# Moving the routing products, the shifted sums and the offset loads in an attention, expert and feed-forward kernel

## The chip, the cores and the metric

The kernel runs on one core of one Trainium2 chip, in one launch. The metric is device time in microseconds (us) of the whole program. Five engines work side by side and wait for one another by semaphores: TensorE (PE, matrix products and transposes; PEld is its weight load), VectorE (DVE), ScalarE (ACT), GpSimd (POOL) and SyncE (SP, which here only issues DMA transfers). A name like PEq, ACTq or SPq is the sequencer of an engine, which issues DMAs and handles registers. PSUM is the memory that PE writes; the kernel uses eight banks of it, tiles of 128 x 512 numbers of 4 bytes.

## The reference

Three steps, each on the output of the one before. Attention, for 4 batches of 8 heads with 576 rows and 64 columns each:

```
s_pos = maximum(s, 0); cum = cumsum(s_pos)
scores = q k^T / 8 + minimum(-(cum_i - cum_j), 0), causal
out = softmax(scores) v
```

Then a routed layer on x, the 2304 tokens of 512 numbers: `logits = x @ w_gate` (8 experts), each token goes to the expert with the greatest logit, `y = gate * (relu(x @ w1[e]) @ w2[e])`, where gate is that expert's softmax share. Then `h = max(y @ m1, y @ m2, y @ m3)` and `out = h @ w_out` for all tokens.

## The kernel before

**Attention** goes over 16 pairs of heads, four pairs to a batch. A pair takes 25 slots of a table (SEQ), and three pairs are in work at once: pair p has its score products (units s0 to s9, line 308, into the banks ps_a, of which there are four, used in turn), pair p-1 its transposes (A0 to TT, line 374, banks ps_b) and its products with the values (v0, v1, line 426, banks ps_c), pair p-2 its rows of the token matrix (x0, x1, lines 459 and 464, tile xr). DVE adds the bias to a score bank and takes the row's extremum (line 314, tile ns), ACT takes the exponential (line 321, tile P), and POOL masks the bias beforehand (line 269).

**The bias** of a pair (tile bl) is made of the running sum cum, shifted. For pair 0 PE spreads cum over the partitions by products with chl, the high and low part of cum (line 236), and the shift is done on DVE and ACT (lines 251 to 255). For all other pairs DVE makes the shifted sums cs once (line 569), SP writes them to DRAM (cumd, lines 575 and 578) and reads them back for each pair, spread over 64 partitions (line 218).

**Routing** of batch b (`route`) starts when the last pair of the batch has its token rows. It is a list C of short operations, one after another: the logits, the greatest (mx), its index (idx), the one-hot matrix oh and its bf16 copy ohb; then products r1 that count, for each token, the tokens before it in its group (bank from ps_a, result read as r_rv); then the place of each token (dd, bb, cbo, caA), and products r3 that put the token numbers in order (bank from ps_a, read into gidx). For the first three batches the list is laid between the attention of later pairs. For the last batch it lies between products of the expert layer, its banks are from ps_b, and its indices gi (line 781) are what POOL's gathers of the routed rows (tile xw, line 915) wait for.

**The expert layer** goes by nine groups of up to 336 tokens. Weights come by SP into tiles wr and xr and are split in a high and a low part (lines 192 and 685). The first three weight tiles are loaded, rounded and split during attention, at places set by WE0, WE1, WES and WEL. Group 0 holds tokens of the first three batches only and fills the time in which the last batch is routed; group 1 needs the gather. The results of groups after 0 go into yT at an offset that ACT holds in registers, loaded by line 793 from offi (`load_offs`).

**The order of the work** is written by hand: every operation is put on one list with `at(slot, fn)`, `atm(us, fn)` being the same by microseconds after the start of group 1, and run_events emits them by rising slot. The slot sets only the order on each engine, and no time: an engine takes its instructions in that order and waits at each for what it needs. `route` puts operation i at `t0 + (RS, RS, RS2, RSL)[b] * i`, that is 1.8, 1.8, 1.6 and 0.6 slots apart.

Of the kernel before, what the change touches and what calls it, by code (L numbers as in the profile page):

```python
# [14 lines left out]
AF = mybir.ActivationFunctionType  # L15
ALU = mybir.AluOpType
# [4 lines left out]
IT = 25  # L21
B, H, S, D = 4, 8, 576, 64
NT, DM, NE, DF, DF2 = B * S, H * D, 8, 1024, 768
P = 128
# [33 lines left out]
BW = 2112  # L58
CST, COT, L1 = -53, -42, -59
T0, T1, T2, T3, T4 = -56, -56, -53, -51, -43  # L60
# [5 lines left out]
MA, MB, MT = 8, 0.5, 0  # L66
RS = 1.8
CL = 26
# [8 lines left out]
WRB, R0, R1, XR, XQ = 3, 3, 2, 2, 1  # L77
WHI = "A"
WLO = "V"
WE0, WE1, WES, WEL, WEH = -62, 80, 46, 3, "A"  # L80
WHE, WLE = "A", "V"
SLOT = 0.456
# [6 lines left out]
LSEQ = "A0 B0 y0 y1 A1 B1 C2 v0 C3 TT . v1 . . x0 x1"  # L89
LS0, LSP, X14, RSL, RS2 = 1, 1.0, 8, 0.6, 1.6  # L90

# [7 lines left out]
def emit(nc, tc, qt, kt, v, s, wg, w1, w2, m64, out, dbg=None):  # L99
    V, A, G, T, SP = nc.vector, nc.scalar, nc.gpsimd, nc.tensor, nc.sync  # L100
# [55 lines left out]
    eio = iota_f([P, 5, NE], [[0, 5], [1, NE]], 0, 0, "eio")  # L156
# [3 lines left out]
    for b in (0, B - 1):  # L160
        t = cp.tile([P, 5, NG], F32, name=f"gx{b}")
# [40 lines left out]
    def at(slot, fn, *args):  # L202
        heapq.heappush(evq, (slot, next(seqno), fn, args))
# [271 lines left out]
    def route(b, t0):  # L475
        z = {}

        def sm(shape, nm, dt=F32):
            z[nm] = ab.tile(shape, dt, tag="r_" + nm, name="r_" + nm, bufs=1)
            return z[nm]  # L480

        b3 = lambda ap: bc(ap.rearrange("p (t o) -> p t o", o=1), (P, 5, NE))
# [3 lines left out]
        C = []  # L486
        op = C.append
# [7 lines left out]
        op(lambda: V.tensor_reduce(sm([P, 5], "mx"), z["L"], AX.X, ALU.max))  # L495
        op(lambda: V.tensor_tensor(sm([P, 5, NE], "ls"), z["L"], b3(z["mx"]), ALU.subtract))
        op(lambda: V.tensor_scalar(sm([P, 5, NE], "val"), z["ls"], 0.0, -float(NE), ALU.is_equal, ALU.mult))
        op(lambda: V.tensor_tensor(z["val"], z["val"], eio, ALU.add))
        op(lambda: V.tensor_reduce(sm([P, 5], "idx"), z["val"], AX.X, ALU.min))
# [14 lines left out]

        C[-1] = lambda: A.activation(sm([P, 5, NE], "ex"), z["ls"], AF.Exp)
        op(r1)
# [20 lines left out]
        def r3():  # L537
            pg = z["pg"] = bank("b" if b == B - 1 else "a")
            for t in range(5):
                T.matmul(pg[:, 0:NGW], z["cbo"][:, t, :], caA[:, NG * NWIN * t:NG * NWIN * t + NGW],  # L540
                         start=(t == 0), stop=(t == 4))

        op(r3)
        op(lambda: V.tensor_tensor(gidx, gidx, z["pg"][:, 0:NG * NWIN], ALU.add))
        if b == B - 1:
            op(lambda: to_idx())

        op(lambda: V.tensor_reduce(sm([P, NG], "os"), oh.rearrange("p t e -> p e t"), AX.X, ALU.add))
        op(lambda: V.tensor_tensor(ocar, ocar, z["os"], ALU.add))
# [3 lines left out]
        op(lambda: V.reciprocal(gtA[:, b], z["se"]))  # L553
        for i, f in enumerate(C):
            at(t0 + (RS, RS, RS2, RSL)[b] * i, f)
        return t0 + (RS, RS, RS2, RSL)[b] * (len(C) - 1)

    pos = {u: x / SLOT for u, x in SEQ.items()}
# [27 lines left out]
    for p in range(NP):  # L586
        t = IT * p
# [25 lines left out]
        if p == NP - 1 - H // 2:  # L613
            TR2 = end
    TA = IT * NP + 4
    TX = max(e[0] for e in evq) + 1
# [3 lines left out]
    def atm(us, fn, *args):  # L620
        at(TM + us / SLOT, fn, *args)
# [23 lines left out]
    t = TE  # L645
    S0, SL = [], []
    for x, gs in enumerate(STEPS):
        if x == NEARLY:
            t = TM
# [110 lines left out]
    for n in range(24):  # L760
        dst = w32 if n < 18 else wo32
        i, x = divmod(n if n < 18 else n - 18, 2)
# [14 lines left out]
    def early_idx():  # L777
        V.tensor_copy(gie, gidx[:, 0:NEARLY * NWIN])

    def to_idx():  # L780
        V.tensor_copy(gi, gidx)
# [109 lines left out]
    XG1 = max(TR2, TA) + 0.2  # L891
    at(TR2 + 0.1, early_idx)
    at(TX + 4, counts)
    at(TX + 8, load_offs)

# [100 lines left out]
    for x, gs in enumerate(STEPS):  # L996
# [7 lines left out]
        for g in gs:  # L1004
            L = cost[g]
            t0 = S0[x] - 1.3 / SLOT - st_ * (4 * len(gs) - m)
# [6 lines left out]
            for kk in range(4):  # L1013
                t = t0 + st_ * kk
# [12 lines left out]
            for d_ in range(4):  # L1027
                t = pt(g, 4 + d_)
# [210 lines left out]
```

## Time and profile before

| | |
|---|---|
| median of 3 runs | 795.99 us (795.22 to 797.65) |
| profiled execution | 794.54 us |
| its span, first to last instruction | 792.8 us |
| mean granted clock of TensorE | 0.995 of full |
| attention, until its last product (line 459) | about 213 us of the span |

The rows below are from that one execution. A timeline row gives the start, the busy time, engine, line, operation with its tiles, and in brackets how long the engine was idle before it and what ended that wait. Starts are in us from the first instruction. A wait is put down to the operation that came last. In a row of windows the granted clock (PEclk) is a share of 2.4 GHz.

### The profile page before, as it was taken

What the parts mean: (1) busy time and instruction counts of PE and PEld (TensorE: products, weight loads), DVE (VectorE), ACT (ScalarE), POOL (GpSimd) and SP (SyncE); (2) the same over time, 40 slices, a digit from 0 to 9 for tenths busy, and PEclk for the clock granted to TensorE, in tenths of its full rate; (3) what the DMA queues carried; (4) which work ended last, traced back from release to release, by engine and by line L of the source; (5) the groups of instructions that cost most, each with busy time, mean ns of one, the idle gap of its engine ahead of it and who ended that gap; (6) DMA issues with size and microseconds to landing.
All of it is one profiled execution on the core that took longest, in us unless ns stands there. A gap on an engine that the chain in (4) does not pass through costs nothing. (4 is left out here: it accounts for less than half of the span.)

```text
span 792.8 us, 12891 instructions
## 1 busy us (share of the span) xinstructions
PE 758.3 (96%) x4782; PEld 681.6 (86%) x4782; DVE 437.1 (55%) x1142; ACT 335.2 (42%) x771; POOL 109.4 (14%) x226
## 2 busy tenths in 40 slices
PE   6999899999889999999999999999999999999996
PEld 4666666666789998999999999989999899898995
DVE  5667757678668686899888756412312223122120
ACT  5666666666546343555455544221121212212111
POOL 3332332333030200101200000010010000100001
PEclk9999999999999999999999999999999999999999
DMA  5887858767386687868776535000010000100001
GB/s 154 238 216 217 212 160 225 194 181 222 135 281 210 221 310 256 308 221 281 238 230 214 204 97 172 26 31 10 1 41 1 26 14 1 41 1 14 26 1 41
DMA packets 34876, 112.43 MB, mean 142 GB/s; under 512 B 4793, under 2 KB 4875, under 8 KB 32891
## 3 DMA queue, kind: packets, MB, share of 16 engines
q1 hardware_dynamic: 24107, 81.66, 34.6%
q10 hardware_dynamic: 7456, 18.89, 6.7%
q0 software_dynamic: 3248, 11.03, 4.1%
q8 instruction: 39, 0.64, 0.3%
q14 instruction: 26, 0.21, 0.1%
HBM read 94.97 MB, written 16.60 MB: 141 GB/s over the span
## 5 line engine op out<-in xcount | busy, mean ns | idle before, releaser
L1135 DVE TENSOR_TENSOR mA<-ps_a,mA 128x384 f32<-128x384 f32 x72 | 40.2, 558 | 181.4 <-PE ps_a L942 181.4
L942 PE MATMUL ps_a<-yc,wq 128*128 128x384 f32 x720 | 129.1, 339 | 0.0
L942 PEld LDWEIGHTS ps_a<-yc,wq 128*128 128x128 f32 x720 | 127.4, 188 | 0.4
L942 PE MATMUL ps_c<-h,wq 128*128 128x336 f32 (+1 forms) x672 | 106.2, 316 | 3.1 <-ACT yT L988 1.6
L942 PEld LDWEIGHTS ps_c<-h,wq 128*128 128x128 f32 x672 | 101.8, 192 | 3.8 <-ACT yT L988 2.0
L942 PE MATMUL ps_a<-yc,wm 128*128 128x384 f32 x576 | 103.7, 339 | 0.0
L942 PE MATMUL ps_a<-xT,wq 128*128 128x336 f32 (+1 forms) x648 | 101.0, 313 | 1.1 <-DVE h L967 1.1
L942 PEld LDWEIGHTS ps_a<-yc,wm 128*128 128x128 f32 x576 | 101.9, 188 | 0.0
L942 PEld LDWEIGHTS ps_a<-xT,wq 128*128 128x128 f32 x648 | 96.5, 188 | 1.7 <-DVE h L967 1.4
L321 ACT ACTIVATE P<-ns,mn 128x512 f32<-128x512 f32 (+3 forms) x128 | 70.6, 558 | 14.9 <-DVE mn L314 14.7
L942 PE MATMUL ps_c<-wm,g 128*128 128x512 f32 x324 | 76.9, 396 | 0.0
L1139 ACT ACTIVATE g<-mA 128x384 fp32r<-128x384 f32 x36 | 18.9, 526 | 135.7 <-DVE mA L1135 135.7
L942 PEld LDWEIGHTS ps_c<-wm,g 128*128 128x128 f32 x324 | 60.9, 188 | 14.4
L1158 POOL DMA_INDIRECT out<-o,midi x18 | 17.5, 973 | 378.1 <-ACT o L1154 373.9
L314 DVE CUSTOM_DVE_ANT_0 ns<-ps_a,bl 128x512 f32<-128x512 f32 (+3 forms) x128 | 57.5, 488 | 19.5 <-PE ps_a L308 8.1
L685 DVE TENSOR_TENSOR wq<-wr,wq 128x1024 fp32r<-128x1024 f32 x44 | 53.9, 1226 | 10.4 <-ACT wq L192 9.7
L426 PEld LDWEIGHTS ps_c<-ptT,nv 128*64 128x64 f32 x448 | 29.8, 138 | 31.5 <-DVE ptT L414 13.3
L426 PE MATMUL ps_c<-ptT,nv 128*64 128x320 f32 (+4 forms) x448 | 51.4, 367 | 5.4 <-DVE ptT L414 5.2
L192 ACT ACTIVATE wq<-wr 128x1024 fp32r<-128x1024 f32 x44 | 46.3, 1056 | 17.9 <-DMA wr<-in_w 17.9
L308 PE MATMUL ps_a<-nk,nq 64*128 64x512 f32 (+3 forms) x256 | 47.0, 472 | 3.4 <-DVE mn L314 1.8
L374 PE MATMUL ps_b<-idf,P 128*128 128x128 f32 x320 | 47.1, 284 | 2.0 <-DVE ptT L414 1.2
L963 ACT ACTIVATE h<-ps_a 128x336 fp32r<-128x336 f32 (+1 forms) x64 | 28.0, 440 | 46.0 <-PE ps_a L942 45.4
(221 smaller groups left out, 953.5 us busy)
## 6 DMA issues: line engine op xcount, KB each, us to landing
wr<-in_w SPq DMA_DIRECT2D x49, 512.0 KB, 4.8
bl<-cumd SPq DMA_DIRECT2D x30, 528.0 KB, 9.1
dr<-in_m ACTq DMA_DIRECT2D x24, 512.0 KB, 4.5
xr<-in_w SPq DMA_DIRECT2D x23, 512.0 KB, 4.8
nq<-in_qt SPq DMA_DIRECT2D x16, 352.0 KB, 3.7
nv<-in_v SPq DMA_DIRECT2D x16, 320.0 KB, 9.5
nk<-in_kt SPq DMA_DIRECT2D x16, 288.0 KB, 2.9
xd<-xr SPq DMA_DIRECT2D x4, 1152.0 KB, 6.5
```

What stands on the lines that cost most here:

```text
L192: A.activation(o, x, AF.Copy)
L308: T.matmul(d["sp", i, g][:, :w], d["q"][r, 128 * i:128 * i + 128], d["k"][r, :w], start=True, stop=True)
L314: V.tensor_tensor_reduce(out=ns[:, :w], in0=d.pop(("sp", i, g))[:, :w], in1=d["bl"][:, 1024 * g + BOFF[i]:1024 * g + BOFF[i] + w], scale=- ...
L321: A.activation(pp, d.pop(("ns", i, g))[:, :w], AF.Exp, bias=d["mn"][:, c:c + 1], scale=-1.0, accum_out=ssum[b][:, i, h + g:h + g + 1])
L374: T.transpose(pt[:, c:c + 128], (d["P", "t"] if g == "t" else d["P", g, i])[:, k0:k0 + 128], idf)
L426: T.matmul(po[64 * g:64 * g + 64, qa - c0:c1 - c0], d["v"][:, g, j], d["pt"][:, g, POFF[j] + qa - 128 * j:POFF[j] + c1 - 128 * j], start=( ...
L685: (V if eng == "V" else G).tensor_tensor(t[:, 1], raws.pop(key), t[:, 0].bitcast(F32), ALU.subtract)
L942: T.matmul(ps_, w_(zw), x_(zx), start=(first and n == 0), stop=(last and n == 2))
L963: A.activation(t[:, 0, :c], hT[n, f, "p"][:, :c], AF.Relu)
L1135: V.tensor_tensor(m, pm[:, :CH], m, ALU.max)
L1139: A.activation(t[:, 0], h2[c, f, "m"], AF.Copy)
L1158: G.indirect_dma_start(out, bass.IndirectOffsetOnAxis(ap=midi[:, n:n + 1].bitcast(U32), axis=0), h2.pop((c, x, "s")), None)
```

## The change

The list `route` makes two operations of three for the index (the test for the greatest logit is made directly on the logits); `ls` and the exponential `ex`, which only the gate needs, come after r3. For the first three batches the slots are chosen so that r1 stands just before the unit x0 of the next pair, and r3 just before the x0 of the pair after; in between the operations are spread evenly, and the conversion of group 0's indices (early_idx) is now part of the list. For the last batch the spacing stays 0.6. The shifted sums cs get an earlier slot (CST), the loads of the first three weight tiles a later one (WE0), and the offset loads move from `TX + 8` to 12 us after the start of group 1.

```diff
-CST, COT, L1 = -53, -42, -59
+CST, COT, L1 = -57, -42, -59
-RS = 1.8
+RS, RX = 1.8, 0.25
-WE0, WE1, WES, WEL, WEH = -62, 80, 46, 3, "A"
+WE0, WE1, WES, WEL, WEH = -23, 80, 46, 3, "A"
...
-        op(lambda: V.tensor_tensor(sm([P, 5, NE], "ls"), z["L"], b3(z["mx"]), ALU.subtract))
-        op(lambda: V.tensor_scalar(sm([P, 5, NE], "val"), z["ls"], 0.0, -float(NE), ALU.is_equal, ALU.mult))
-        op(lambda: V.tensor_tensor(z["val"], z["val"], eio, ALU.add))
+        op(lambda: V.tensor_tensor(sm([P, 5, NE], "val"), z["L"], b3(z["mx"]), ALU.is_equal))
+        op(lambda: V.scalar_tensor_tensor(z["val"], z["val"], -float(NE), eio, ALU.mult, ALU.add))
...
-        C[-1] = lambda: A.activation(sm([P, 5, NE], "ex"), z["ls"], AF.Exp)
+        R1 = len(C)
         op(r1)
...
+        R3 = len(C)
         op(r3)
         op(lambda: V.tensor_tensor(gidx, gidx, z["pg"][:, 0:NG * NWIN], ALU.add))
         if b == B - 1:
             op(lambda: to_idx())
-
+        if b == B - 2:
+            op(lambda: early_idx())
+
+        op(lambda: V.tensor_tensor(sm([P, 5, NE], "ls"), z["L"], b3(z["mx"]), ALU.subtract))
+        op(lambda: A.activation(sm([P, 5, NE], "ex"), z["ls"], AF.Exp))
...
-        for i, f in enumerate(C):
-            at(t0 + (RS, RS, RS2, RSL)[b] * i, f)
-        return t0 + (RS, RS, RS2, RSL)[b] * (len(C) - 1)
+        if b == B - 1:
+            ts = [t0 + RSL * i for i in range(len(C))]
+        else:
+
+            a = t0 + (pos["x0"] - RX / SLOT - t0) % IT
+            a = a if a > t0 + 1.2 * R1 else a + IT
+            ts = [t0 + (a - t0) / R1 * i for i in range(R1)] + \
+                [a + (IT / (R3 - R1)) * i for i in range(R3 - R1)] + [a + IT + RS * i for i in range(len(C) - R3)]
+        for t, f in zip(ts, C):
+            at(t, f)
+        return ts[R3 + 2]
...
-    at(TR2 + 0.1, early_idx)
     at(TX + 4, counts)
-    at(TX + 8, load_offs)
+    atm(12, load_offs)
```

On DVE at the start of the program stood, before (chl is the high and low part of cum, cs the shifted sums for DRAM, bl the bias of pair 0, sh the amount of a shift):

```order
L134 TENSOR_SCALAR chl<-cum 32x576
L135 TENSOR_TENSOR chl<-cum,chl 32x576
L251 TENSOR_SCALAR bl<-ps_a 128x256
L254 TENSOR_SCALAR sh<-ps_a 128x1
L569 TENSOR_SCALAR cs<-cum 32x256
L569 TENSOR_SCALAR cs<-cum 32x512
L569 TENSOR_SCALAR cs<-cum 32x576
L251 TENSOR_SCALAR bl<-ps_a 128x256
```

and now:

```order
L134 TENSOR_SCALAR chl<-cum 32x576
L581 TENSOR_SCALAR cs<-cum 32x256
L135 TENSOR_TENSOR chl<-cum,chl 32x576
L581 TENSOR_SCALAR cs<-cum 32x512
L581 TENSOR_SCALAR cs<-cum 32x576
L251 TENSOR_SCALAR bl<-ps_a 128x256
L254 TENSOR_SCALAR sh<-ps_a 128x1
L251 TENSOR_SCALAR bl<-ps_a 128x256
```

All three cs now stand ahead of the first bias operation, and the first of them ahead of the low part of chl.

On PE around r3 of the first batch (line 540, now 539) stood, before, where line 308 is the scores, 374 the transposes and 459 the token rows:

```order
L308 MATMUL ps_a<-nk,nq 128x512 x2
L308 MATMUL ps_a<-nk,nq 128x256 x2
L540 MATMUL ps_a<-caA,r_cbo 128x28 x5
L374 MATMUL ps_b<-idf,P_1227 128x128
L374 MATMUL ps_b<-idf,P_1276 128x128
L374 MATMUL ps_b<-idf,P_1211 128x128
L374 MATMUL ps_b<-idf,P_1229 128x128
L374 MATMUL ps_b<-idf,P_1278 128x128
L374 MATMUL ps_b<-idf,P_1213 128x128
L459 MATMUL ps_c<-rh,oT 128x144 x5
L308 MATMUL ps_a<-nk,nq 128x384 x2
L308 MATMUL ps_a<-nk,nq 128x128 x2
```

and now:

```order
L308 MATMUL ps_a<-nk,nq 128x512 x2
L308 MATMUL ps_a<-nk,nq 128x256 x2
L374 MATMUL ps_b<-idf,P_1225 128x128
L374 MATMUL ps_b<-idf,P_1273 128x128
L374 MATMUL ps_b<-idf,P_1214 128x128
L374 MATMUL ps_b<-idf,P_1227 128x128
L374 MATMUL ps_b<-idf,P_1275 128x128
L374 MATMUL ps_b<-idf,P_1216 128x128
L539 MATMUL ps_a<-caA,r_cbo 128x28 x5
L459 MATMUL ps_c<-rh,oT 128x144 x5
L308 MATMUL ps_a<-nk,nq 128x384 x2
L308 MATMUL ps_a<-nk,nq 128x128 x2
```

The five small products went from ahead of six transposes to behind them. In the same way r1 went from between the two parts of line 459 to ahead of both.

On DVE in the routing of the third batch, where r1's result is read (r_rv) beside the copies of the transposes and the token rows, stood, before:

```order
L414 COPY ptT<-ps_b 128x384
L517 TENSOR_TENSOR r_rv<-ps_a,ohA 128x45
L414 COPY ptT<-ps_b 128x384
L464 TENSOR_TENSOR xr<-ps_c,rc 128x3x144
L519 TENSOR_REDUCE rkA<-r_rv 128x5
L464 TENSOR_TENSOR xr<-ps_c,rc 128x2x144
```

and now:

```order
L414 COPY ptT<-ps_b 128x384 x2
L464 TENSOR_TENSOR xr<-ps_c,rc 128x3x144
L516 TENSOR_TENSOR r_rv<-ps_a,ohA 128x45
L464 TENSOR_TENSOR xr<-ps_c,rc 128x2x144
L518 TENSOR_REDUCE rkA<-r_rv 128x5
```

Here the read of r1 moved back behind the second copy and the first part of the token rows. In the first two batches it stood behind both parts before, and now stands at this same place.

## Rows read from the trace of the kernel before

**Rows 1.** The page's first part: busy time, share of the span, instructions

```profile
PE 758.3 (96%) x4782; PEld 681.6 (86%) x4782; DVE 437.1 (55%) x1142; ACT 335.2 (42%) x771; POOL 109.4 (14%) x226
```

**Rows 2.** The chain that ended last, its first long piece: start, us, what

```profile
466.58 15.04 PE ps_c L942 x96
```

**Rows 3.** Waits of PE, whole span: us in total, times, longest

```profile
PE ps_a L540 <- DVE mn L314: 2.1, 2, 1.7
PE ps_a L308 <- DVE r_rv L517: 1.6, 2, 0.8
```

**Rows 4.** Timeline of all engines, start of the program

```profile
5.42 0.75 DVE L135 TENSOR_TENSOR chl<-cum,chl 32x576 fp32r<-32x576 f32 x1
...
7.05 0.49 DVE L251 TENSOR_SCALAR bl<-ps_a 128x256 f32<-128x256 f32 x1 [0.89 <-PE ps_a L236]
...
7.52 1.16 DVE L569 TENSOR_SCALAR cs<-cum 32x256 f32<-32x256 f32 x3
...
8.28 1.31 SPq L575 DMA_DIRECT2D cumd<-cs  x2
...
12.49 1.14 SPq L218 DMA_DIRECT2D bl<-cumd  x2
...
16.50 0.43 SPq L677 DMA_DIRECT2D wr<-in_w  x1
...
20.03 0.63 POOL L269 TENSOR_SCALAR_AFFINE_SELECT bl<-bl 128x512 f32<-128x512 f32 x1 [6.24 <-DMA bl<-cumd]
...
20.70 0.69 DVE L314 CUSTOM_DVE_ANT_0 ns<-ps_a,bl 128x512 f32<-128x512 f32 x1 [2.90 <-POOL bl L269]
...
21.45 1.80 PE L308 MATMUL ps_a<-nk,nq 64*128 64x384 f32 x8 [1.83 <-DVE mn L314]
```

**Rows 5.** Windows: length, busy times, then granted clock, DMA share, GB/s

```profile
23.00:27.00 4.00, 4.00 (x22) 2.79 (x22) 2.10 (x10) 3.50 (x13) 0.89 (x4) 0.57 1.04 224
```

**Rows 6.** Timeline of PE, routing of the first batch

```profile
84.36 0.46 PE L308 MATMUL ps_a<-nk,nq 64*128 64x128 f32 x2 [0.80 <-DVE r_rv L517]
...
94.79 0.73 PE L540 MATMUL ps_a<-caA,r_cbo 128*128 128x28 f32 x5 [1.66 <-DVE mn L314]
95.36 0.88 PE L374 MATMUL ps_b<-idf,P 128*128 128x128 f32 x6
96.08 1.39 PE L459 MATMUL ps_c<-rh,oT 128*128 128x144 f32 x10
```

**Rows 7.** Timeline of DVE, the same routing

```profile
83.14 0.97 DVE L464 TENSOR_TENSOR xr<-ps_c,rc 128x432 f32<-128x432 f32 x2
84.01 0.20 DVE L517 TENSOR_TENSOR r_rv<-ps_a,ohA 128x45 f32<-128x45 f32 x1
...
94.03 0.69 DVE L314 CUSTOM_DVE_ANT_0 ns<-ps_a,bl 128x512 f32<-128x512 f32 x1
```

**Rows 8.** Timeline of PE, routing of the second and third batch

```profile
143.04 0.73 PE L540 MATMUL ps_a<-caA,r_cbo 128*128 128x28 f32 x5 [0.45 <-DVE mn L314]
...
181.27 0.88 PE L374 MATMUL ps_b<-idf,P 128*128 128x128 f32 x6
```

**Rows 9.** Timeline of DVE, third batch: r_rv, then the first token rows

```profile
180.29 0.20 DVE L517 TENSOR_TENSOR r_rv<-ps_a,ohA 128x45 f32<-128x45 f32 x1
...
180.87 0.60 DVE L464 TENSOR_TENSOR xr<-ps_c,rc 128x432 f32<-128x432 f32 x1
```

**Rows 10.** Timeline of PE: last gathered rows of group 1, second layer of group 1

```profile
233.49 0.58 PE L921 MATMUL ps_b<-idf,xw 80*128 80x80 f32 x4 [1.07 <-DMA xw<-xd,gi]
...
256.59 7.55 PE L942 MATMUL ps_c<-h,wq 128*128 128x336 f32 x48
```

**Rows 11.** Instructions of the tile gi on DVE: ns min/median/max, start

```profile
L781 DVE CAST gi<-gidx x1: 178/178/178, 223.2 to 223.2; 128x27 int32<-128x27 f32 x1
```

**Rows 12.** Offset loads (tile offi): ns min/median/max, first and last start

```profile
L793 ACTq TENSOR_LOAD <-offi x8: 271/278/478, 230.0 to 232.6; - x8
```

**Rows 13.** Timeline of ACT: the last eviction of h in group 1

```profile
256.79 0.45 ACT L963 ACTIVATE h<-ps_a 128x336 fp32r<-128x336 f32 x1 [1.39 <-PE ps_a L942]
```

More of the change, by code (lines that the diff above doesn't have):

```diff
@@ L89 @@
 LSEQ = "A0 B0 y0 y1 A1 B1 C2 v0 C3 TT . v1 . . x0 x1"
-LS0, LSP, X14, RSL, RS2 = 1, 1.0, 8, 0.6, 1.6
+LS0, LSP, X14, RSL = 1, 1.0, 8, 0.6
 SEQ = {"A0": 0, "B0": 0.45, "s0": 0.9, "s1": 0.9, "s2": 1.95, "s3": 1.95, "A1": 2.65, "B1": 3.0, "x0": 3.35, "x1": 4.15,
```

## The prediction

> **What bounds the kernel now.** I read the page's busy times first: PE works 758.3 of 792.8 us [rows 1], so what can be won is mostly its 34.5 us of idle time, and an engine beside it is worth something only where PE waits for it. The chain of waits comes second. From 466.58 us to the end it is matrix products in unbroken rows [rows 2], and no line of the change works there. Third, the list of PE's waits for whole lines, and for each of them the timeline around it. Three places touch the change. One is at the start: PE stands 1.83 us before 21.45, for the scores of pair 1 [rows 4], and from 23 to 27 us the granted clock is 0.57, in parts at the lower of its two levels, 1.2 GHz [rows 5]. One is the routing: r3 waits 2.1 us in two waits, and the scores wait 1.6 us in two waits for r_rv [rows 3]. The last is the gathered rows of group 1, whose last wait ends at 233.49 [rows 10].
>
> **The start.** At 21.45 PE needs a bank that DVE frees at 20.70 plus its 0.69; DVE waited for POOL's mask, and POOL for the bias transfer to land, after 6.24 us idle [rows 4]. So the transfer ends last. It is issued at 12.49, after the DRAM copy of cs, whose first part is issued at 8.28, when two of the three cs operations are done; DVE makes these from 7.52 on [rows 4]. Now they stand ahead of the bias operation at 7.05, before which DVE idled 0.89 us. The three take 1.16 us; by their widths 256, 512 and 576 the first takes about 0.28. It delays the low part of chl from 5.42 to 5.70, which then ends at about 6.45; the second cs ends at about 6.85, so the copy to DRAM is issued at about 6.9 instead of 8.28, 1.4 us sooner. With everything after it as long as now, the bias lands 1.35 us sooner, DVE starts at 19.35, PE at 20.1. Pair 0 pays 0.28 for the delay on PE, but wins it back, since its other bias operations no longer stand behind cs; I count 0. Bounds for this step: minus 0.3 (the transfer lands when it does now, and pair 0 is late) to plus 1.8 (the whole wait).
>
> With less of a wait the clock may not fall. Four microseconds at 0.57 cost 0.43 x 4 = 1.7 us of work [rows 5]; the waits of 1.66 us in the routing are longer than the 0.5 us or so that would remain at 21 us, and the trace shows 1.66 us of idle at 94.79 without a group of slow products behind it (six transposes in 0.72, from 95.36 to 96.08 [rows 6]). I take 1.2 of the 1.7, since ACT's exponentials would then be what the next transposes wait for; bounds 0 and 1.7. The Trainium skill (TensorE: Matmul & The Clock Gate, Part 1: The HAM clock gate) says that the place of such a change differs from run to run. By it the fall could stay even with the shorter wait, which is the first rival below.
>
> The first weight load leaves its place at 16.50 [rows 4], behind the bias of pair 1 in SP's queue and ahead of that of pair 2. All three go to places where SP issues a later one now, still well ahead of the rounding; I count 0 for them.
>
> **The routing products.** PE's banks ps_a are used in turn, so r1 lends its bank to the fourth score product after it. In the first batch that product waits until 84.36, for r_rv, which DVE starts at 84.01, behind both token row operations from 83.14 (0.87 us) [rows 6, 7]. Now r_rv stands between them, 0.36 us sooner by their widths 432 and 288, and the copy ohb (about 0.1) has left the scores of DVE: 0.46 us. The second batch has the same wait (0.8 each, 1.6 in two [rows 3]): 2 x 0.46 = 0.9 us. In the third batch r_rv ran already at 180.29, before the token rows, and no wait is listed. Now it comes behind the first of them, 180.87 less 0.1 plus 0.51: it ends at 181.5, and the product that had ended by 181.27 can start only then and take its 0.4 [rows 8, 9], which is the length of such a product in [rows 6]. That costs 0.7 us.
>
> r3 takes the bank of the first score product, which DVE frees 0.7 us after 94.03; PE stood 1.66 us before it at 94.79 [rows 6, 7]. Six transposes, 0.72 us, now go first and fill this much of the wait: 0.7 us. In the second batch the wait of 0.45 [rows 8] is filled wholly: 0.45. In the third r3 had no wait. The read gidx moves behind two copies, and its bank is wanted by the fourth score product after it; by the same rows (copies of about 0.45 each after four score operations from 94.03) it is free at about 97.5, and the product comes at 97.6. That cover is thin, 0.1 us, and if it is gone a few tenths are lost in each batch. Sum: 0.9 + 0.7 + 0.45 - 0.7 = 1.35, say 1.4; bounds 0.4 and 2.5. The two small operations fewer and the later ls and ex lie on engines that wait there.
>
> **The last batch.** ohb now stands ahead of a weight split of over a microsecond, so r1 no longer waits. But gidx and gi are again parted by an operation of the expert layer: adding up the new order with the lengths of now, gi ends at 223.35, as before [rows 11]. The gather starts when it did, and 233.49 [rows 10] stays: 0, bounds minus 0.5 and plus 0.8.
>
> **The offset loads.** Eight register loads stand from 230.0 to 232.9 on ACT's sequencer [rows 12], and end before the rows of group 1 come at 233.49, so taking them away brings nothing now. At the new place they stand ahead of the last eviction of h, at 256.79 [rows 13], and hold it for at most 2.9 us, more likely 1.1, since the engine had idled 1.39 before. The second layer starts at 256.59 and takes 7.55 us for 48 products; that h comes into the last three of its first 24, at about 256.6 + 0.875 x 3.8 = 259.9. Cover: with 0.45 for the eviction and as much for the split, it is ready at 258.9. Cost 0; if the cover is gone, up to 0.7 on that product alone. The Trainium skill (DMA: Bandwidth & Descriptors, Latency and other measured facts) gives a tensor_load a floor of about 600 ns. By it eight would take 4.8 us, and a loss of some 2 us would follow here; the trace has 278 ns in the middle [rows 12], and I go by that.
>
> **Sum.** 1.35 + 1.2 + 1.4 = 3.95, say 4.0 us. The profiled execution took 794.54 us, which makes 790.5; it was 1.45 below the median, so by the median 795.99 - 4.0 = 792.0.
>
> **Rivals.**
> - The clock falls all the same. The scores come sooner, but PE still idles about a microsecond in all before 23 us. 4.0 - 1.2 = 2.8: 793.2.
> - The bias doesn't land sooner. The DMA share is 1.04 from 23 to 27 us [rows 5], so the engines are full then; if what is issued sooner only queues longer, the wait and the fall stay. For it speaks that 7.5 us pass from issue to landing [rows 4], against it that little else is queued at 12 us. Left is the routing: 1.4, 794.6.
> - The routing products don't do what is said: r_rv and gidx on DVE now stand later than the bank is wanted, and what r3 wins is lost behind it. Then only the start is left: 2.55, 793.4.
> - Slower: the offset loads stop the expert layer. Place: group 1, between its last evictions. Sequencer and engine behind are late by the whole 2.9 us, h and then the weight rounding behind it, PE stands that long, and the clock falls as at 23 us (1.7). 2.9 + 1.7 = 4.6 against 4.0 won: 796.6. It decides as soon as the last h is ready more than 2 us after 259.9. Against it: ACT idled 1.39 us there.
>
> **How the numbers follow.** Forecast 0.52; clock falls 0.15; bias as before 0.14; routing without gain 0.11; slower 0.08. A measurement of this kernel tells 0.3%, 2.4 us, from no change. The forecast and the rivals of 2.8 and 2.55 us are beyond that mostly, the other two not. Faster: 0.52 x 0.9 + 0.15 x 0.6 + 0.11 x 0.55 + 0.14 x 0.2 = 0.65; slower than by 0.3% is only the worse part of the last rival and what I have not seen, 0.06; same 0.29. The range goes from 789.0 (every step at its upper bound: 1.8 + 1.7 + 2.5 = 6.0, and one more for the gather) to 795.5, which takes in the bias as before and leaves out the slower case.
>
> **What would show it.** In the profile after: SP's first write of cumd near 6.9 and POOL's first mask of a transferred bias near 18.7; PE's wait for the scores of pair 1 under 1 us; the granted clock near 1.00 from 22 to 27 us; r_rv's two waits at about 0.35 and a third one new in batch three; r3's waits at 0.9 and none; the gathered rows still waited for some 2.8 us; no wait of PE for h behind the offset loads. I am wrong if the mask still starts at 20 us, if DVE's copies or gidx appear among PE's waits for 1 us or more, or if PE stands at the start of the second layer of group 1.

## The result: 804.4 us, slower by 1.05%

| | median | lowest to highest | runs |
|---|---|---|---|
| before | 796.61 us | 794.50 to 798.03 | 6 |
| after | 804.44 us | 801.60 to 807.87 | 6 |

The ratio is 1.0105, with a 95% interval of 1.0076 to 1.0135. Forecast were 792.0 us and a range of 789.0 to 795.5. The profiled execution after took 801.6 us (span 799.9), so it lies 2.8 under its own median. Against the 792.8 of before it is 7.1 us longer.

The page's first part shows PE busy 4.7 us longer for the same 4782 instructions [rows 1]:

```profile
PE 763.0 (95%) x4782; PEld 685.6 (86%) x4782; DVE 436.9 (55%) x1142; ACT 335.4 (42%) x771; POOL 110.8 (14%) x226
```

More busy time for the same work points to the clock, and the other 2.4 us of the 7.1 must be idle time. PE's waits in the profile after, in us in total, times and longest, that changed or that the forecast spoke of:

```profile
PE ps_b L374 <- ACT ptT L416: 3.9, 2, 3.7
PE ps_b L932 <- DMA xw<-xd,gi: 2.9, 2, 1.5
...
PE ps_a L308 <- DVE mn L314: 1.7, 1, 1.7
...
PE ps_a L308 <- DVE r_rv L516: 1.1, 3, 0.4
PE ps_b L932 <- issue: 1.0, 1, 1.0
...
PE ps_a L539 <- DVE mn L314: 0.4, 1, 0.4
```

The first line was 0.2 before, and is now 3.9, with one wait of 3.7. The wait of 1.7 for mn looks like the 1.83 of [rows 4] but is a new one, at 46 us; the old one is gone. Two lines of [rows 3] are answered well: the waits for r_rv fell from 1.6 to 1.1, though three now, and r3's from 2.1 to 0.4. The gathered rows are still waited for, 3.9 us with the third wait, which the profile puts down to the issue, against 2.8 before.

**Where the loss arises.** A mark is the start of the same product in both traces; the difference is after minus before, in us, minus for sooner:

| mark (its time before) | after | loads back | loads alone | sums alone | routing alone | loads mid |
|---|---|---|---|---|---|---|
| first scores of pair 2 (31.27) | -2.5 | -3.5 | -1.5 | -3.4 | -0.3 | -3.3 |
| pair 4 (54.42) | +1.9 | -3.5 | +3.8 | -3.4 | -0.3 | -3.3 |
| pair 6 (78.67) | +6.0 | -3.8 | +8.1 | -3.3 | -0.6 | -3.6 |
| pair 8 (105.28) | +4.9 | -4.8 | +8.1 | -3.3 | -1.6 | -4.3 |
| pair 12 (153.53) | +4.1 | -5.8 | +8.1 | -3.3 | -2.3 | -5.3 |
| first transpose of group 0's rows (205.77) | +5.1 | -4.9 | +8.1 | -3.3 | -0.9 | -4.3 |
| last gathered rows of group 1 (233.49) | +6.0 | -3.7 | +8.5 | -2.9 | -0.0 | -3.4 |
| span (792.8) | +7.1 | -1.7 | +12.4 | +2.0 | +2.2 | -0.3 |

The other columns are the experiments e1, e2, e3, e4 and e7, told below. Each column is one execution, compared with one of the kernel before; of 29 executions of the kernel before beside e1 the times go from 792.7 to 798.6, so a microsecond or two at a late mark can be chance. In the column after, the kernel is 2.5 us ahead at pair 2, loses 4.4 by pair 4 and 4.1 more by pair 6, and wins 1.1 back in the routing of the first batch. Both losses have the same shape. The timeline of ACT after shows a rounding of a weight tile that waits for its load while ACT has other work behind it:

```profile
44.03 1.06 ACT L192 ACTIVATE wq<-wr 128x1024 fp32r<-128x1024 f32 x1 [2.85 <-DMA wr<-in_w]
45.00 0.70 ACT L321 ACTIVATE P<-ns,mn 128x512 f32<-128x512 f32 x1
...
71.13 1.06 ACT L192 ACTIVATE wq<-wr 128x1024 fp32r<-128x1024 f32 x1 [3.38 <-DMA wr<-in_w]
72.09 1.07 ACT L416 ACTIVATE ptT<-ps_b 128x512 f32<-128x512 f32 x2
```

ACT stands 2.85 and 3.38 us, and the exponentials P (first wait) and the copies ptT (second) come behind the rounding, in ACT's order. In the timeline of ACT before, the first of these roundings has no wait:

```profile
43.55 1.07 ACT L192 ACTIVATE wq<-wr 128x1024 fp32r<-128x1024 f32 x1
```

The timeline of SP after shows when the loads were issued:

```profile
36.75 0.33 SPq L213 DMA_DIRECT2D nk<-in_kt  x1
37.13 0.42 SPq L213 DMA_DIRECT2D nq<-in_qt  x1
37.61 0.42 SPq L689 DMA_DIRECT2D wr<-in_w  x1
...
65.15 2.03 SPq L689 DMA_DIRECT2D wr<-in_w  x1
```

The load stands behind the keys and queries of a pair, nk and nq, which SP issues only when PE has freed their buffers. SP's waits after, from 20 to 90 us, have this as their longest by far:

```profile
SPq L213 <- PE ps_a L328: 47.1, 5, 12.9
```

So the first load is issued at 37.61. ACT is ready for it at 44.03 - 2.85 = 41.18, only 3.6 us later, and it has landed 6.4 us after its issue. The second is issued at 65.15 and its rounding starts 6.0 us later. In the kernel before the first load was issued at 16.50 [rows 4]. The timeline of PE after, behind the two stops:

```profile
46.31 0.49 PE L308 MATMUL ps_a<-nk,nq 64*128 64x128 f32 x2 [1.74 <-DVE mn L314]
...
48.65 0.44 PE L374 MATMUL ps_b<-idf,P 128*128 128x128 f32 x2 [0.94 <-DVE ptT L414]
...
72.72 1.39 PE L374 MATMUL ps_b<-idf,P 128*128 128x128 f32 x6 [3.70 <-ACT ptT L416]
```

PE waits 1.74 us for DVE's score operations, which wait for the exponentials to give buffers back, then 0.94 for a copy, and later 3.70 us for ptT. In the windows of after (length, busy times, then granted clock, DMA share, GB/s) the clock falls behind both:

```profile
23.00:27.00 4.00, 4.00 (x31) 2.38 (x31) 2.61 (x13) 3.20 (x12) 0.00 (x0) 1.00 0.87 187
48.00:53.00 5.00, 4.35 (x19) 2.91 (x19) 3.98 (x14) 3.24 (x12) 1.15 (x4) 0.66 0.08 28
73.00:78.00 5.00, 5.00 (x28) 4.17 (x27) 4.88 (x16) 2.66 (x9) 1.46 (x5) 0.66 0.54 115
```

A clock of 0.66 over five us is a loss of 0.34 x 5 = 1.7 us each time. For the first stop that makes 1.74 + 0.25 (a short wait at 47.05) + 0.94 + 1.7 = 4.6; less the 0.5 that PE waited there before it is 4.1, against 4.4 at the marks. For the second it makes 3.70 + 0.54 (a wait at 81.40) + 1.7 = 5.9; less the 1.5 of three waits there before (0.21, 0.25 and 1.07) it is 4.4, against 4.1. The first line of the windows is the good news: from 23 to 27 us the clock stands at 1.00, where it was 0.57 [rows 5]; how much of that the change has done is taken up below, under the start.

### The profile page after: what moved, and what is told of

It reads as the page before. It is cut to its first block, busy times and chain, and to the rows that moved or that the text cites. A ratio compares the mean times of both kernels' runs of the same rounds, so it can differ in the third digit from the quotient of the medians.

```text
span 799.9 us, 12890 instructions
## 1 busy us (share of the span) xinstructions
PE 763.0 (95%) x4782; PEld 685.6 (86%) x4782; DVE 436.9 (55%) x1142; ACT 335.4 (42%) x771; POOL 110.8 (14%) x226
## 5 line engine op out<-in xcount | busy, mean ns | idle before, releaser
L426 PEld LDWEIGHTS ps_c<-ptT,nv 128*64 128x64 f32 x448 | 29.8, 138 | 31.0 <-DVE ptT L414 12.6
L374 PEld LDWEIGHTS ps_b<-idf,P 128*128 128x128 f32 x320 | 35.1, 143 | 15.1 <-ACT ptT L416 9.1
```

Source lines behind the costliest of these rows:

```text
L374: T.transpose(pt[:, c:c + 128], (d["P", "t"] if g == "t" else d["P", g, i])[:, k0:k0 + 128], idf)
L426: T.matmul(po[64 * g:64 * g + 64, qa - c0:c1 - c0], d["v"][:, g, j], d["pt"][:, g, POFF[j] + qa - 128 * j:POFF[j] + c1 - 128 * j], start=( ...
```

## The experiments

All times are medians with the kernel before run beside them on the same chip. There the kernel before took 794.1 to 795.7 us, not the 796.6 from which the expectations in microseconds were set, so these are better compared by the ratio.

| label | what it is | us | before | ratio | 95% |
|---|---|---|---|---|---|
| e1_loads_back | after, loads at their old place | 793.09 | 794.87 | 0.9981 | 0.9966 to 0.9996 |
| e2_loads_alone | before, loads at their new place | 807.44 | 794.87 | 1.0185 | 1.0152 to 1.0218 |
| e6_round_late | after, roundings 14 slots later | 793.12 | 794.87 | 0.9982 | 0.9962 to 1.0002 |
| e7_loads_mid | after, loads one pair sooner | 792.58 | 794.87 | 0.9969 | 0.9954 to 0.9985 |
| e3_sums_alone | before, sums sooner | 794.70 | 795.70 | 0.9984 | 0.9963 to 1.0005 |
| e4_routing_alone | before, new routing | 795.57 | 795.70 | 1.0001 | 0.9985 to 1.0016 |
| e5_offs_back | e1, offset loads at their old place | 793.64 | 795.70 | 0.9977 | 0.9959 to 0.9995 |
| e8_gather_sooner | e7, last batch's routing tighter | 791.26 | 795.70 | 0.9952 | 0.9933 to 0.9971 |
| e10_gather_alone | before, last batch's routing tighter | 795.92 | 795.55 | 1.0010 | 0.9993 to 1.0027 |
| e9_loads_later | after, loads later still | 811.32 | 795.55 | 1.0198 | 1.0168 to 1.0227 |
| e11_index_sooner | e7, cast gi ahead of one h | 790.93 | 794.11 | 0.9959 | 0.9937 to 0.9981 |

### e1_loads_back

```diff
-WE0, WE1, WES, WEL, WEH = -23, 80, 46, 3, "A"
+WE0, WE1, WES, WEL, WEH = -62, 80, 46, 3, "A"
```

> The changed kernel with the first three weight loads back at their old places in SP's queue; the order on the other engines is that of the changed kernel. Theory A: the roundings of these loads on ACT wait for them (2.85 us to 44.03 and 3.38 us to 71.13 in the profile after), and everything behind them in ACT's order, so the loads' new place costs all of the two steps between the profiles (from 2.5 us ahead to 1.9 behind, and from 1.9 to 6.0 behind: 4.4 + 4.1 = 8.5 us). Then this kernel takes 804.4 - 8.5 = 796.0, between 794 and 797.5, ACT waits for no wr before 215 us, and TensorE's clock stays at 1.00 from 46 to 77 us. Rival B: ACT and DVE are late there by what the routing and the sooner sums moved, and the load is only the last of several waits: then over 801. Rival C: the load costs at its old place as well, by standing in the way of the bias of pairs 1 and 2, and the start gives 1 us or more of its 2.5 us back: 797.5 or more.

Only the places of these loads in SP's order change, and the kernel goes from slower to slightly faster than before. ACT has no wait for wr before 215 us, and the marks of pairs 2, 4 and 5 stand at -3.5 throughout. The median of 793.1 lies 0.9 below the range of theory A; by the ratio it is 795.1 at the 796.6 of before, inside it. Theory A holds. Rival C falls with it, since the start keeps its whole gain with the load at 16 us. The timeline of PE, start of this kernel:

```profile
19.46 1.77 PE L308 MATMUL ps_a<-nk,nq 64*128 64x384 f32 x8
21.21 0.90 PE L374 MATMUL ps_b<-idf,P 128*128 128x128 f32 x6
```

The scores of pair 1 start at 19.46, without a wait, where [rows 4] has 21.45 with 1.83.

### e2_loads_alone

```diff
-WE0, WE1, WES, WEL, WEH = -62, 80, 46, 3, "A"
+WE0, WE1, WES, WEL, WEH = -23, 80, 46, 3, "A"
```

> The kernel before with only the first three weight loads at their new places. Theory A: 796.6 + 8.5 = 805, between 802 and 807, with the two waits of ACT for wr of about 3 us each near 44 and 68 us; the score and routing waits of the kernel before remain. Rival B: within 2 us of the kernel before.

The one number alone makes the kernel before slower by 12.6 us. That is more than theory A has: 807.4 is 0.4 us over its upper end, and by the ratio (811.3) it is 4.3 over. ACT's waits from 30 to 215 us, and PE's in the whole span:

```profile
ACT wq L192 <- DMA wr<-in_w: 6.6, 2, 3.5
```

```profile
PE ps_b L374 <- ACT ptT L416: 3.8, 1, 3.8
PE ps_c L942 <- ACT yT L988: 3.4, 1, 3.4
```

The two stops cost 5.3 and 4.2 us between the marks of pairs 2, 4 and 6. Most of the rest comes behind 300 us: a wait of 3.4 us for yT, which is 1.6 at most in the profiles of before and after, with a clock of 0.66 from 320 to 330 us behind it. e3, which leaves the loads where they were, has this wait as well, so it is not shown to be the loads' doing.

### e6_round_late

```diff
-WE0, WE1, WES, WEL, WEH = -23, 80, 46, 3, "A"
+WE0, WE1, WES, WEL, WEH = -37, 94, 46, 3, "A"
```

> The changed kernel with the loads where it has them, but the three roundings (and the subtractions behind them) 14 slots, 6.4 us, later in the plan. The longest wait was 3.38 us, so theory A says that the waits go: 796.0, between 794 and 798, like the kernel with the loads back. If the load's place itself does the harm (it fills the DMA engines when the bias of pairs 4 and 6 is to come, rival C), the time stays over 801.

SP's order is that of the changed kernel: the first load is issued at 36.77 here and at 37.61 there. Only the roundings and what hangs on them are later (the first at 47.51, without a wait), and the loss is gone: by the ratio 795.2, in the range given. So what cost the time was the distance between load and rounding, not the load's place among the transfers.

### e7_loads_mid

```diff
-WE0, WE1, WES, WEL, WEH = -23, 80, 46, 3, "A"
+WE0, WE1, WES, WEL, WEH = -40, 80, 46, 3, "A"
```

> The changed kernel with the loads one pair sooner in SP's queue (17 slots in the plan), one pair later than in the kernel before for the first two. The first is issued near 26.5 us and lands near 33 us by the 6.4 us that it took, 8 us ahead of its rounding. Theory A: the same as with the loads back, 796.0, between 793.5 and 797.5; if the start also gains by the first load's absence at 16 us, up to 1 us less than that kernel. Rival B: over 801.

The first load is issued at 25.68, its rounding starts at 40.22 without a wait. By the ratio the time is 794.1, in the range of theory A, and it is that of e1 within the intervals; that it is faster than e1 is not shown.

### e9_loads_later

```diff
-WE0, WE1, WES, WEL, WEH = -23, 80, 46, 3, "A"
+WE0, WE1, WES, WEL, WEH = -14, 80, 46, 3, "A"
```

> The changed kernel with the first three loads 9 slots later still in the plan, which puts each behind the keys and queries of one more pair in SP's queue. Theory A: SP comes to a load only when PE has freed the buffers of that pair, while ACT stands at the rounding; each of the two waits of 2.85 and 3.38 us grows by several us (the next pair's keys were issued 15.6 us behind the first load), as far as PE and DVE get without ACT: 3 to 8 us each, so 810 to 822. If the loads are not the cause, within 2 us of the changed kernel (804.4).

The premise held for one load only: the first two kept their place in SP's order, and the third alone went behind one more pair's keys and queries. The time is in the range given, but the reading is another. The timelines of ACT and of SP in this kernel:

```profile
44.25 1.06 ACT L192 ACTIVATE wq<-wr 128x1024 fp32r<-128x1024 f32 x1 [4.11 <-DMA wr<-in_w]
...
73.14 1.06 ACT L192 ACTIVATE wq<-wr 128x1024 fp32r<-128x1024 f32 x1 [4.89 <-DMA wr<-in_w]
...
102.67 1.06 ACT L192 ACTIVATE wq<-wr 128x1024 fp32r<-128x1024 f32 x1 [3.08 <-DMA wr<-in_w]
```

```profile
36.57 0.42 SPq L689 DMA_DIRECT2D wr<-in_w  x1
...
65.66 0.42 SPq L689 DMA_DIRECT2D wr<-in_w  x1
...
96.99 1.27 SPq L213 DMA_DIRECT2D nq<-in_qt  x1
98.32 0.42 SPq L689 DMA_DIRECT2D wr<-in_w  x1
```

The third rounding, which had no wait in the profile after, now waits 3.08 us, and the marks lose 4.7 us between pairs 7 and 8, where the kernel after wins 0.6: 5.3 us for one load made late. The first two waits are longer too (4.11 and 4.89), with the load in the same place. At the first PE was 1.0 us further ahead than in the profile after, and these loads took 7.7 and 7.5 us from their issue to their rounding, 6.4 and 6.0 there; the third took 4.4.

### e3_sums_alone

```diff
-CST, COT, L1 = -53, -42, -59
+CST, COT, L1 = -57, -42, -59
```

> The kernel before with only the shifted sums made sooner. In the kernel with the loads back PE is 3.5 us ahead at the scores of pair 2 (27.75 against 31.27). Theory D: the sooner sums alone do that, since the bias of pair 1 lands 2 us sooner and the clock does not fall at 23 us: 3 to 3.5 us ahead at pair 2 and until the transition, and up to 1 us of it lost at the gather: 1.0 to 3.5 us under the kernel before, ratio 0.9955 to 0.9985. Rival E: whatever is won before 205 us is lost again behind it, since the gathered rows land when the DMA engines are through with the weights: within 0.8 us of the kernel before.

The marks are as theory D has them: 3.4 ahead at pair 2, 3.3 at 205 us, 2.9 at the last gathered rows. The median is only 1.0 us lower, at the lower end of what D has, and its interval takes in 1 and rival E's 0.8 us, so the time does not decide between them. The profiled execution shows one way in which such a lead is lost. PE's timeline, and the window around it:

```profile
311.79 5.50 PE L942 MATMUL ps_c<-h,wq 128*128 128x336 f32 x24 [3.44 <-ACT yT L988]
```

```profile
310.00:320.00 10.00, 8.21 (x49) 8.20 (x50) 5.28 (x12) 4.36 (x8) 0.00 (x0) 0.83 0.82 289
```

A wait of 3.44 us for yT, which stands on ACT behind two roundings that wait for wr, is 1.9 longer than the same wait in the profile before (1.55), and the clock of 0.83 takes 0.17 x 10 = 1.7 us more: 3.6 of the 4.9 us that lie between 2.9 ahead at the gathered rows and a span 2.0 us longer than before. How often an execution has it, one profile each cannot say.

### e4_routing_alone

The edit is that of `route` in the change, with the other three parts as before.

> The kernel before with the routing of the changed kernel alone (places of its products and the fewer operations): sums, loads and offset loads as before. From the marks of the kernel with the loads back: 0.25 + 0.45 + 0.6 in the first batch, 0.5 + 0.5 in the second, minus 0.3 in the third, so 2.0 us ahead at 190 us. Theory F: of these, 0.6 to 2 us are lost between 190 and 300 us, where the rows of group 1 land later against their index (11.0 us behind the first gather against 9.9) and the second step's order on DVE is another one: 0 to 1.4 us under the kernel before, ratio 0.998 to 1.0005. Rival: the 2 us stay, ratio 0.9975 or less.

Theory F holds: 2.3 us ahead at pair 12, 0.9 at 205.77, nothing at the last gathered rows, and the same time. The fall from 2.3 to 0.9 lies in the third batch (1.0 in e1 and e7), where the forecast had a loss of 0.7. Of the 0.9, 0.3 stood at pair 2 already, ahead of all routing.

### e5_offs_back

```diff
-    atm(12, load_offs)
+    at(TX + 8, load_offs)
```

> The kernel with the loads back, and the eight offset loads at their old place on ACT as well. The order differs in nothing else. My forecast counted 0 for this move and no wait of PE behind the loads was found: within 0.8 us of the kernel with the loads back (793.1). Rival: the loads' new place, in the middle of the first layer of group 1, is part of the 1.3 us lost between the gathered rows and 279 us: then 1 us or more faster than that kernel.

The same as e1 (ratios 0.9977 and 0.9981). No cost of the offset loads shows at either place, and PE has no wait behind them; the intervals leave room for about 2 us either way.

### e8_gather_sooner and e10_gather_alone

Both have this edit, e8 on top of e7, e10 on top of the kernel before (there the first line also sets RS2, to 1.6 on both sides):

```diff
-LS0, LSP, X14, RSL = 1, 1.0, 8, 0.6
+LS0, LSP, X14, RSL = 1, 1.0, 8, 0.5
...
-        op(lambda: V.tensor_tensor(gidx, gidx, z["pg"][:, 0:NG * NWIN], ALU.add))
-        if b == B - 1:
-            op(lambda: to_idx())
+        def gidx_gi():
+            V.tensor_tensor(gidx, gidx, z["pg"][:, 0:NG * NWIN], ALU.add)
+            if b == B - 1:
+                to_idx()
+
+        op(gidx_gi)
```

> The kernel with the loads one pair sooner, and the last batch's routing in steps of 0.5 instead of 0.6 slots with the cast to the index right behind the sum: on PE the last routing product goes 12 products (1.5 us) further ahead, on DVE its input ahead of a weight split. Theory G: the gather starts 1.5 to 2 us sooner and PE's wait for its rows (3.7 us in the profile of that kernel) shrinks to about 2; if the clock falls less as well, 1 us more: 789.5 to 791.5. Rival E: the rows land when the DMA engines have moved the weights that were asked for before them; then the wait stays and the time is 792.6 within 0.7.

> The kernel before with only the last batch's routing in steps of 0.5 slots and the cast to the index right behind its sum (the two edits that took the kernel with the loads one pair sooner from a ratio of 0.9969 to 0.9952). If theory G is right, that the last routing product 12 products further ahead brings the gathered rows sooner, it holds in the kernel before as well: the gather starts at about 222 instead of 223.62, PE's wait for its rows shrinks from 2.8 us to about 1.5, 1 to 2 us faster, ratio 0.9975 to 0.9990. Rival E, that the rows land when the DMA engines are through with the weights: the wait stays at 2.5 us or more and the time within 0.6 us.

In e10 the gather starts 0.9 us sooner against the products around it, the waits for its rows fall from 2.8 to 2.4, and the time does not change: theory G is not borne out there. In e8 what it says comes out: the waits for the rows fall from 3.7 to 2.3, and the median of 791.3 lies in G's range and under E's (by the ratio 791.1 at the 794.9 that before took beside e7). But its interval overlaps that of e7, and its last gathered rows come at 229.91, those of e7 at 230.05; PE came to this stretch 0.6 us later, which is part of the shorter wait. e8 has the lowest profiled time of all (span 786.4), 3.1 us under its own median, while the profile of e7 is 1.8 over its own. One thing that differs in the two profiles is the clock behind the gather. Windows of e7 and then of e8:

```profile
225.00:230.00 5.00, 1.38 (x8) 0.72 (x6) 0.00 (x0) 1.06 (x1) 1.84 (x2) 0.78 1.00 355
230.00:235.00 5.00, 4.95 (x25) 4.95 (x26) 3.94 (x6) 2.70 (x5) 0.00 (x0) 0.54 1.01 371
```

```profile
230.00:235.00 5.00, 5.00 (x44) 5.00 (x45) 4.16 (x8) 3.88 (x8) 0.00 (x0) 1.00 1.03 370
```

From 230 to 235 us e7 runs at 0.54, e8 at 1.00: 2.3 us of work. Of the 6.1 us between the two spans 2.2 are there at 264 us; behind it PE waits 3.2 us for yT in e7 and 1.1 in e8. One profile of each does not show whether the edit or chance made these differences. By the ratio e8 is the fastest version that was run, 0.3 to 0.7% under the kernel before, with e11 (below) beside it; what either has over e7 is not told apart from none.

### e11_index_sooner

The edit is the second half of the one above, on top of e7.

> The kernel with the loads one pair sooner, and only the cast gi right behind gidx on DVE, ahead of one operation of h, with the steps left at 0.6 slots. In the kernels with the changed routing the first gather's issue on POOL begins 0.11 us into one of DVE's 1.22 us weight splits and takes 1.98 us instead of 0.99; with the cast sooner an operation of h and three small ones stand between it and that split. Theory H, that the issue waits for the split's end: it takes 1.0 us now, the second gather starts 1.3 to 1.5 us sooner against the products around it, and the 0.85 us that the kernel loses between 205 us and the last gathered rows shrink to 0.4 or less; 791.5 to 792.3 in all. If the length of that first issue has another reason, it stays at 1.98. Rival E, that the rows land when the DMA engines have moved the weights: the issue is shorter, and the last wait still ends where it does now (230.05), the time 792.6 within 0.7.

Theory H is right on the issue and wrong on what it is worth: the loss up to the last gathered rows stays at 0.8 us, where it has 0.4 or less. Gathers on POOL and the operations of DVE ahead of them in the kernel after, and POOL's first gather in e11:

```profile
228.56 1.98 POOL L926 DMA_INDIRECT xw<-xd,gi  x1 [20.92 <-DVE r_os L552]
```

```profile
228.12 0.17 DVE L793 CAST gi<-gidx 128x27 int32<-128x27 f32 x1
...
228.45 1.22 DVE L697 TENSOR_TENSOR wq<-wr,wq 128x1024 fp32r<-128x1024 f32 x1
```

```profile
219.76 1.03 POOL L929 DMA_INDIRECT xw<-xd,gi  x1 [21.76 <-DVE gi L796]
```

The first issue begins 0.11 us into a weight split and takes 1.98 us; in e11, where it begins 0.43 us ahead of one, it takes 1.03. The first rows gain by that: they land 3.6 us behind the issue, against 7.6 in e7, and PE has no wait before them (1.33 in e7). But the last rows come at the same time, in e7 and in e11:

```profile
230.05 0.95 PE L932 MATMUL ps_b<-idf,xw 80*128 80x80 f32 x4 [1.30 <-DMA xw<-xd,gi]
```

```profile
230.08 0.58 PE L935 MATMUL ps_b<-idf,xw 80*128 80x80 f32 x4 [1.81 <-DMA xw<-xd,gi]
```

So rival E has the landing of the last rows. The DMA share is 1.00 from 225 to 230 us in e7 and e11, and 1.01 to 1.03 in the five us behind: the engines are full there, mostly with weights. The time decides nothing: 790.9 is under both ranges, by the ratio it is 791.6, at the 794.9 that before took beside e7, and in the range of theory H, and the interval overlaps that of e7.

## Why the prediction was wrong

**The step that failed** is the one on the weight loads: "All three go to places where SP issues a later one now, still well ahead of the rounding; I count 0 for them." This is a fourth part of the change, which the title does not name. The price was 8.5 us at the marks (4.4 + 4.1), and 9.6 by the medians (e1 is 1.8 under its before, the changed kernel 7.8 over). No time was worked out for the distance, only the order. The constant -23 is 23 slots of 0.456 us, 10.5 us in the plan; but the load stands behind keys and queries that wait for PE, so 3.6 us were left when ACT was ready, and the transfer took 6.4. Rows that would have told it were at hand: the bias needed 7.5 us from issue to landing [rows 4], and SP's place behind a pair's keys fixes the earliest issue. The rival that went to the slower side had the right mechanism, an engine held in order with evictions behind it and a clock that falls after, and the wrong place.

**The start** was right in direction: 2.55 forecast, 3.1 to 3.5 against this profile in e1, e3, e5, e6, e7 and e8. It has two terms. The earlier landing was sized too small: 1.35 forecast with 1.8 at most, and the scores of pair 1 that started at 21.45 start at 19.46 in e1 and 19.51 in e3, 2.0 sooner. The clock's 1.2 came out as 1.5 (3.5 less 2.0), but part of that is the luck of the one profile it is compared with. e2 and e10 have the old sums, and PE waits as long there, but the clock does not fall and they are 1.5 and 1.6 ahead at pair 2 with nothing changed at the start. PE's timeline and a window of e2:

```profile
21.48 1.80 PE L308 MATMUL ps_a<-nk,nq 64*128 64x384 f32 x8 [1.91 <-DVE mn L314]
```

```profile
23.00:27.00 4.00, 4.00 (x30) 2.67 (x30) 3.08 (x13) 4.00 (x15) 0.92 (x4) 1.00 0.93 203
```

Of the four profiles with the old start two have the fall (before, and e4 with 0.64 after a wait of 1.76), and of the nine with the sooner sums none. So the 2.0 us are won in any case here; the other 1.5 are won only where the kernel before has the fall.

In the profile after, SP and POOL stand where they were expected, or sooner (6.9 and 18.7 were forecast). The timelines of SP and POOL, then of PE:

```profile
6.61 1.31 SPq L587 DMA_DIRECT2D cumd<-cs  x2
...
10.21 1.14 SPq L218 DMA_DIRECT2D bl<-cumd  x2
```

```profile
18.02 0.64 POOL L269 TENSOR_SCALAR_AFFINE_SELECT bl<-bl 128x512 f32<-128x512 f32 x1 [4.31 <-DMA bl<-cumd]
```

```profile
16.60 1.92 PE L374 MATMUL ps_b<-idf,P 128*128 128x128 f32 x8
...
20.74 1.51 PE L308 MATMUL ps_a<-nk,nq 64*128 64x384 f32 x8
```

The scores of pair 1 that waited 1.83 us [rows 4] start at 20.74, as soon as the transposes ahead of them are through, and the clock does not fall. That the profile after is only 2.5 ahead at pair 2 is in its first row: eight transposes in 1.92 us, against 1.06 before and 1.07 and 1.06 in e1 and e3. At 0.24 us each they are about as slow as six from 23.24 in the profile before (1.54 us, 0.26 each), where the clock is 0.57, so PE was most likely still at the lower level of its clock there.

**The routing products** were about right: 1.4 forecast, 1.3 in e1, 1.0 in e7 and 0.6 in e4 (from pair 2 to 205.77). By batches e1 wins 1.3 and 1.0 and loses 1.0, where 1.16, 0.91 and a loss of 0.7 were forecast. In the timeline of PE after, the wait for r_rv stands at 0.36 in the first and, new, in the third batch, as forecast, and r3's at 0.41 where 0.9 was forecast:

```profile
89.88 0.46 PE L308 MATMUL ps_a<-nk,nq 64*128 64x128 f32 x2 [0.36 <-DVE r_rv L516]
...
100.30 0.73 PE L539 MATMUL ps_a<-caA,r_cbo 128*128 128x28 f32 x5 [0.41 <-DVE mn L314]
...
185.71 0.46 PE L308 MATMUL ps_a<-nk,nq 64*128 64x128 f32 x2 [0.36 <-DVE r_rv L516]
```

**The last batch and behind.** I counted 0 for it, with 0.8 at most. The kernels with the new routing lose 0.6 to 1.4 us between 205.77 and the last gathered rows (e1, e4, e5, e6, e7, and after with 0.9; only e8, which comes there late, loses 0.1), the sums alone lose 0.4. e11 loses 0.8 as well, without the slow first issue, so that is not the cause. Nor is it that a lead is waited away there: after comes to this stretch 5.1 us late and e9 13.2 late, and both lose 0.9, while with the old routing e3, 3.3 ahead, and e2, 8.1 late, lose 0.4 each. So far as these runs go, the loss goes with the new routing and not with the lead. In e1 PE stands longer (4.1 against 2.8 us in all for these rows) and then runs slower for longer; the windows of e1, against 0.98 from 230 to 235 and 0.68 from 235 to 240 us before:

```profile
225.00:230.00 5.00, 0.89 (x5) 0.51 (x5) 0.00 (x0) 0.56 (x1) 1.52 (x2) 0.91 0.96 350
230.00:235.00 5.00, 5.00 (x25) 5.00 (x25) 3.96 (x6) 2.71 (x5) 0.00 (x0) 0.50 1.03 366
235.00:240.00 5.00, 5.00 (x40) 5.00 (x39) 2.24 (x5) 2.17 (x5) 0.26 (x1) 0.90 0.40 122
```

From 225 to 240 us the clock takes 1.7 us of work in the profile before (5 x (0.02 + 0.32)) and about 3.4 in those of e1, e5, e6 and e7; in e3, e4 and e11 it takes 1.7, in e8 nothing. So of 4.9 us ahead at 205.77, e1 keeps 1.7 at the end of the span; its median is 1.8 lower. What in the new routing makes the rows late, and what is lost behind them, is not settled.

**The offset loads**: 0 forecast, none seen within the interval (e5). No wait of PE stands behind them.

With the loads one pair sooner the changed kernel takes 2.3 us less than before, where I had 4.0 for all parts. Up to 205.77 us the terms come to 4.3 against this one profile, but up to 1.5 of that is a fall of the clock that the kernel before does not always have, and up to 1.4 is lost at the gather.

## What to carry to other kernels

When a load is moved later, compare times, not places: the issue can't be sooner than the last wait ahead of it in its queue, and the landing follows a measured transfer time behind it. If the consumer's engine works in order, a load that is late by 3 us stops everything behind the consumer, and here each such stop cost 4 to 5 us with the clock that fell after it. A lead at a mark is measured against one execution: of e3's 3.4 us about 1.5 was a clock that had fallen in the profile it was compared with, and its median is 1.0 lower. So small gains need the times of many executions, and several profiles of the kernel before, not a mark in one trace.

## What the runs showed of the hardware

- An indirect gather's issue on POOL takes 0.90 to 1.08 us mostly, but 1.85 to 1.98 when it begins 0.11 to 0.17 us into one of DVE's weight splits (1.22 us, two inputs in SBUF), 1.64 when 0.36 into it and 1.15 when 0.88 into it: it ends about 0.8 us behind the split. An issue that begins within 0.02 us of the split takes 0.91 to 0.99. The Trainium skill (SBUF — State Buffer, Who interferes with whom) says that a DVE instruction with two inputs in SBUF and a GpSimd instruction that reads SBUF contend for one read interface, and that the order of issue decides which of them blocks. The rows agree for the gather. For the split no run shows it: one that begins 0.1 to 0.7 us into a gather's issue takes its 1.22 us all the same.
- The granted clock was 0.66 over five us behind PE's waits of 1.74, 0.25 and 0.94 us between 44 and 49 us, and behind one of 3.70 us. Behind a wait of 1.76 to 1.91 us that ends between 21.2 and 21.5 us it was 0.57 and 0.64 over four us in before and e4, and 1.00 in e2 and e10, with the same work ahead of it. In e8 it stayed at 1.00 behind 1.36 and 0.97 us at the gather.
- 512 KB of weights took 4.4 to 7.7 us from issue to the start of the waiting rounding (after, e2, e9), with a pair's keys, queries and bias under way beside them. In the kernel before such loads into wr took 5.9 to 7.5 us to land when issued between 10 and 70 us, and 3.6 to 11.2 between 215 and 240 us, where the DMA share reaches 1.02.
